# A fused attention and SwiGLU backward: the fourth ds tile of each block transposed by DMA from step 160, and the plain transfers issued from GpSimd

## The chip, the cores and the metric

One core of a Trainium2 chip runs the kernel. The metric is the device time of one execution in microseconds (us), as the median of several runs. Engines are named PE (TensorE matmul), PEld (its weight loads), DVE (VectorE), ACT (ScalarE), POOL (GpSimd) and SP (SyncE, which in this kernel does nothing but issue DMA).

## The reference, cut to what matters

```python
# x: 2048 tokens x 448, 16 heads of 28; the vjp gives six gradients beside the output
xn = layernorm(x)
out = x + attention(xn, wqkv, wo) + (silu(xn @ w_gate) * (xn @ w_up)) @ w_down
# backward of attention, per head:
#   ds = p * (dp - delta);  dq = ds @ k;  dk = ds.T @ q
```

The part that matters is the backward of the attention scores. The product ds comes out with query rows on the partitions. The dk sum can use it like that, but the dq sum needs it transposed.

## The kernel before

The backward is one loop of 512 steps. A step handles one query tile of 128 rows against 512 keys for two heads; four steps are a block. Between these steps PE works on other matmuls (the output, the FFN gradients, the weight gradients), which need plain loads that are "dripped" in.

```python
    def drop():                       # plain loads, paced over the steps
        ...
        while slow and credit > 0:
            _, _, o, i = slow.pop(0)
            SP.dma_start(out=o, in_=i)
            credit -= size(o)
...
    def dst_dma(b, ds, qi):           # one query tile, 128 x 1024 bf16, by DMA
        if qi == 0:
            dsT[b] = bk.tile([P, 4, 2, 4, P], BF16, name="dsT", bufs=3)
        SP.dma_start_transpose(out=dsT[b][:, qi].rearrange("p j kt s -> p (j kt) s"),
                               in_=ds[:].rearrange("p j k -> p (j k)"))

    def ew(k):                        # exponentials on ACT, ds on DVE
        ...
            if qi < 2 or qi == 2 and b < NB // 4 - 1:
                ...
                    dst_dma(b, ds, qi)
...
    def tr_unit(b):                   # the fourth tile: PE transposes, ACT copies
        for qi in (3,) if b < NB // 4 - 1 else (2, 3):
            ds = dss.pop(4 * b + qi)
            ps = ps_b.tile([P, 8, P], BF16, name="db", bufs=3)
            for c in range(8):
                PE.transpose(ps[:, c, :], ds[:, c // 4, (c % 4) * P:(c % 4 + 1) * P], ident_bf[:])
            ...
                ACTE.copy(out=o, in_=ps[:])
...
    def dq_unit(b):                   # reads dsT[b], nine steps after the block's last ds
        ...
        ACTE.mul(out=st[:], in_=ps[:, :256], mul=SCALE)
        if kc < 3:
            POOL.tensor_tensor(out=dq_acc[:, qsl], in0=dq_acc[:, qsl], in1=st[:], op=ALU.add)
```

So three tiles of each block are transposed by DMA from SyncE, the fourth by PE and ACT. SyncE also issues every plain load; GpSimd issues the stores and adds up dq.

The softmax here doesn't subtract the row's maximum and nothing guards it: scores larger than these inputs give would overflow.

## Time and profile before

| | before |
|---|---|
| median of 4 runs | 1445.22 us |
| span of the profiled run | 1440.1 us |
| steps 160 to 511 ("the stretch") | 860.68 to 1394.87 us, 534.2 us |
| after the stretch (tail) | 45.2 us |

The stretch is bounded by the first exponential of step 160 and the end of the last ds product. The page's first part gives busy time and share of the span per engine, its third part what each DMA queue moved (packets, MB, share of 16 engines). The lines that the prediction shows follow further down.

```profile
PE 1326.3 (92%) x12647; PEld 541.0 (38%) x12708; DVE 1151.8 (80%) x1997; ACT 1261.5 (88%) x2193; POOL 403.6 (28%) x561
...
q1 hardware_dynamic: 672576, 255.35, 87.1%
q0 software_dynamic: 7024, 13.82, 4.1%
```

Queue q1 is SyncE's and q0 is GpSimd's. The "issue" of a transfer is the time for which the instruction that starts it holds the issuing engine; the transfer "lands" later, when its data have arrived. SyncE is not in the first part, since issuing DMA is not counted as busy.

### The profile page before, as it was taken

Reading aid. Unit: us, or ns where it says so; the run is one execution under the profiler, and the core shown is the slowest. Engines: PE = TensorE matmul, PEld = TensorE weight load, DVE = VectorE, ACT = ScalarE, POOL = GpSimd, SP = SyncE. Lnnn points to the kernel's source line nnn. Section 1 sums busy time; section 2 is a strip of 40 time slices with the busy share of each in tenths; the row PEclk is TensorE's granted clock in tenths of the full one; section 3 lists DMA queues with packets and bytes.
Section 4 is the critical chain, followed back from the end, with each engine's and each line's share of the span. In section 5 each row is a group of like instructions: output and inputs, shape, how many; then the busy total and the mean of one; then the engine's idle time right before and its main releaser. Section 6 shows DMA issues by size and latency. Waiting matters only on the chain. (4 is left out here: it accounts for less than half of the span.)

```text
span 1440.1 us, 34682 instructions
## 1 busy us (share of the span) xinstructions
PE 1326.3 (92%) x12647; PEld 541.0 (38%) x12708; DVE 1151.8 (80%) x1997; ACT 1261.5 (88%) x2193; POOL 403.6 (28%) x561
## 2 busy tenths in 40 slices
PE   5889999999999999889999999999999999999996
PEld 2333333333333333333333434433443444444343
DVE  6667757666676676578998998888889999989988
ACT  5789988988889999869989989899989999989974
POOL 6464524464334454111112112201111011010006
PEclk9999999999999999989999999999999999999998
DMA  5796956796678586799999999999999999999971
GB/s 154 181 199 165 235 122 160 187 195 164 146 162 192 147 172 145 178 234 226 226 213 217 232 220 188 196 209 229 228 173 194 209 223 230 201 191 203 198 142 60
DMA packets 681179, 271.69 MB, mean 189 GB/s; under 512 B 606424, under 2 KB 655824, under 8 KB 681008
## 3 DMA queue, kind: packets, MB, share of 16 engines
q1 hardware_dynamic: 672576, 255.35, 87.1%
q0 software_dynamic: 7024, 13.82, 4.1%
q8 instruction: 100, 1.64, 0.5%
q14 instruction: 71, 0.58, 0.1%
q10 hardware_dynamic: 1408, 0.30, 0.1%
HBM read 65.09 MB, written 60.36 MB: 87 GB/s over the span
## 5 line engine op out<-in xcount | busy, mean ns | idle before, releaser
L842 DVE TENSOR_TENSOR ds_sb<-db,e_sb 128x512 bf16<-128x512 f32 x1024 | 646.8, 684 | 51.3 <-issue 21.1
L836 ACT ACTIVATE e_sb<-sb 128x512 bf16<-128x512 f32 x1024 | 554.8, 611 | 60.4 <-PE db L820 44.5
L612 ACT ACTIVATE eT<-s_w 128x1024 bf16<-128x1024 f32 x256 | 263.5, 1029 | 46.1 <-PE s_ps L609 43.1
L614 ACT ACTIVATE eT<-s_ps 128x512 bf16<-128x512 f32 x512 | 280.4, 612 | 0.0
L820 PE MATMUL db<-kd,qd 32*128 32x512 bf16 x1024 | 234.4, 384 | 8.2 <-DVE ds_sb L842 7.4
L812 PE MATMUL sb<-kd,qd 32*128 32x512 bf16 x1024 | 210.4, 387 | 5.1 <-DMA qd<-QD_d 3.3
L961 POOL TENSOR_TENSOR dq_acc<-dq_acc,dq_st 128x256 f32<-128x256 f32 x64 | 46.2, 721 | 455.4 <-ACT dq_st L959 455.4
L919 PE MATMUL acc<-ds_sb,qd 128*32 128x512 bf16 x1024 | 161.0, 391 | 0.0
L915 PE MATMUL acc<-e_sb,qd 128*32 128x512 bf16 x1024 | 158.8, 391 | 1.3 <-DVE dw_o L528 1.3
L902 ACT COPY dsT<-db 128x1024 bf16<-128x1024 bf16 x128 | 130.1, 1016 | 14.6 <-PE db L897 13.9
L380 POOL TENSOR_TENSOR nn<-nn,ag 128x512 f32<-128x512 f32 x56 | 71.2, 1271 | 252.2 <-DVE ag L378 243.7
L609 PE MATMUL s_ps<-QQ,KK 32*128 32x512 bf16 x512 | 125.4, 385 | 3.9
L1128 PE MATMUL genb<-wguT,dau_c 128*128 128x448 bf16 x448 | 117.5, 355 | 6.3 <-ACT dq_st L959 3.9
L609 PE MATMUL s_w<-QQ,KK 32*128 32x512 bf16 x512 | 100.3, 387 | 13.1 <-ACT eT L612 10.4
L812 PEld LDWEIGHTS <-qd 32*128 32x128 bf16 x1024 | 48.2, 91 | 149.4 <-issue 140.3
L421 PE MATMUL gen<-xn_t,f_sp 128*128 128x448 bf16 x416 | 91.8, 354 | 2.6 <-DVE nn L395 1.7
L421 PEld LDWEIGHTS <-f_sp 128*128 128x128 bf16 x640 | 55.7, 98 | 75.0 <-issue 31.9
L946 PE MATMUL genb<-dsT,kd 128*32 128x256 bf16 x2048 | 79.5, 275 | 1.9 <-DVE dqT L955 0.6
L897 PE MATMUL db<-ident_bf,ds_sb 128*128 128x128 bf16 x1032 | 79.4, 220 | 1.1 <-DVE ds_sb L842 1.1
L897 PEld LDWEIGHTS <-ds_sb 128*128 128x128 bf16 x1032 | 68.3, 99 | 24.1 <-issue 5.3
L451 PE MATMUL gen<-eT,VS 128*32 128x512 bf16 x1024 | 68.4, 384 | 5.5 <-DVE nn L395 3.3
L381 POOL TENSOR_TENSOR nn<-nn,tt 128x512 f32<-128x512 f32 x56 | 72.0, 1286 | 4.4
(167 smaller groups left out, 1911.0 us busy)
## 6 DMA issues: line engine op xcount, KB each, us to landing
F_d<-hda SPq DMA_DIRECT2D x56, 384.0 KB, 3.1
dau_c<-F_d SPq DMA_DIRECT2D x24, 512.0 KB, 4.4
qd<-QD_d SPq DMA_DIRECT2D x16, 512.0 KB
kd<-KD_d SPq DMA_DIRECT2D x16, 384.0 KB, 4.0
dsT<-ds_sb SPq DMA_TRANSPOSE x383, 4.3
dc<-dqkvT_d SPq DMA_DIRECT2D x12, 384.0 KB, 3.9
h_c<-F_d SPq DMA_DIRECT2D x8, 512.0 KB, 4.4
wT_d<-wT_f SPq DMA_DIRECT2D x14, 256.0 KB, 3.6
```

The costliest lines, as they stand in the source:

```text
L421: PE.matmul(ps[:, :D], lhsT=fsp[fc][:, t // 4, w, t % 4, :], rhs=rhs[:, t, :], start=(t == 0), stop=(t == NT - 1))
L609: PE.matmul(sp4[hh], lhsT=KK[g][r:r + HP, kt * P:(kt + 1) * P], rhs=QQ[g][r:r + HP, qsl], start=True, stop=True, tile_position=(r, 0))
L612: ACTE.activation(out=e2[0][:], in_=wide[:], func=ACT.Exp, scale=SCALE)
L614: ACTE.activation(out=e2[1][:, j], in_=sp4[2 + j], func=ACT.Exp, scale=SCALE)
L812: PE.matmul(s_ps[:], lhsT=qside[g, qc][r:r + HP, 0, qi * P:(qi + 1) * P], rhs=kside[g, kc][r:r + HP, 0, :], start=True, stop=True, tile_po ...
L820: PE.matmul(d_ps[:], lhsT=qside[g, qc][r:r + HP, 1, qi * P:(qi + 1) * P], rhs=kside[g, kc][r:r + HP, 1, :], start=True, stop=True, tile_po ...
L836: ACTE.activation(out=est[k][:, j], in_=sps.pop((k, j))[:], func=ACT.Exp, scale=SCALE)
L842: DVE.tensor_tensor(out=ds[:, j], in0=dps.pop((k - 1, j))[:], in1=est[k - 1][:, j], op=ALU.mult)
L897: PE.transpose(ps[:, c, :], ds[:, c // 4, (c % 4) * P:(c % 4 + 1) * P], ident_bf[:])
L902: ACTE.copy(out=o, in_=ps[:])
L915: PE.matmul(a[r:r + HP, :], lhsT=sp4[:, 1, r:r + HP], rhs=e[:, j, :], start=first, stop=last, tile_position=(0, r), skip_group_check=True)
L919: PE.matmul(a[r:r + HP, :], lhsT=sp4[:, 0, r:r + HP], rhs=ds[:, j, :], start=first, stop=last, tile_position=(0, r), skip_group_check=True)
```

## The change

The intent is to take 87 tiles off PE and ACT, which are nearly full, and give them to the DMA path. To make room in SyncE's queue, all plain loads from step 160 on are issued by GpSimd. As GpSimd would run ahead in stretches without sums, a tiny copy ("tie") makes it wait for ACT there.

```diff
-            SP.dma_start(out=o, in_=i)
+            (SP if now < 160 else POOL).dma_start(out=o, in_=i)
... (the same once more, in have())
+    PB = 40
+
+    def by_pe(b):
+        return (3,) if b < PB else (2, 3) if b == NB // 4 - 1 else ()
...
-            if qi < 2 or qi == 2 and b < NB // 4 - 1:
+            if qi not in by_pe(b):
...
-        for qi in (3,) if b < NB // 4 - 1 else (2, 3):
+        for qi in by_pe(b):
...
         if kc == 0:
             ACTE.mul(out=dq_acc[:, qsl], in_=ps[:, :256], mul=SCALE)
+            if now >= 160:
+                POOL.tensor_copy(out=tie[:], in_=dq_acc[0:1, qsl.start:qsl.start + 1])
             return
```

More of the change, by code (lines that the diff above doesn't have):

```diff
@@ L774, in have @@
             slow.remove(x)
-            SP.dma_start(out=x[2], in_=x[3])
+            (SP if now < 160 else POOL).dma_start(out=x[2], in_=x[3])
     def load_q(g, qc):
@@ L888, in late_dw @@
         yield 110
+    tie = bk.tile([1, 1], FP32, name="tie", bufs=1)
     dq_acc = bk.tile([P, S // 2], FP32, name="dq_acc", bufs=1)
     def tr_unit(b):
-        for qi in (3,) if b < NB // 4 - 1 else (2, 3):
+        for qi in by_pe(b):
             ds = dss.pop(4 * b + qi)
@@ L910, in kv @@
         e = est.pop(k)
-        ds = dss[k] if qi == 3 or k == NB - 2 else dss.pop(k)
+        ds = dss[k] if qi in by_pe(k // 4) else dss.pop(k)
         sp4 = qside[g, qc][:, 2:4, qi * P:(qi + 1) * P]
```

## The prediction

> **What bounds the kernel now.** I read the page first, then the busy time by stretch, then the groups of the stretch that the change touches, then the transposes' own view, then SyncE's queue. The chain of waits is of no use here: it holds only the last microsecond of the tail. The exponentials of the backward (line L836, two per step, 512 steps) place the steps in time: step 160 starts at 860.69 us and the last step ends at about 1393.40 us. The change acts only there, on 352 steps, that is 88 blocks of four query tiles, 532.71 / 88 = 6.05 us per block. Busy time by stretch (PE, PEld, DVE, ACT, POOL, clock, DMA share, GB/s), the whole stretch and then two pieces of 16 steps:
>
> ```profile
> 860.69:1393.40 532.71, 511.96 (x5868) 215.71 (x5867) 487.08 (x825) 489.80 (x913) 68.87 (x103) 0.99 1.08 202
> ...
> 961.10:985.60 24.50, 23.33 (x265) 9.65 (x266) 20.28 (x33) 23.35 (x46) 3.42 (x5) 1.00 1.13 207
> ...
> 1155.90:1179.20 23.30, 22.74 (x262) 9.28 (x263) 22.17 (x37) 22.03 (x41) 3.42 (x5) 1.00 1.13 238
> ```
>
> Three engines are nearly full together: PE 96%, ACT 92%, DVE 91%; in the piece at 1155.9 us DVE and ACT both stand at 95% and PE at 98%. The DMA share is above 1 because times of overlapping packets are added; it says "hardly ever idle". The groups of the same stretch, line engine op, count | busy, mean ns | idle before:
>
> ```profile
> L842 DVE TENSOR_TENSOR ds_sb<-db,e_sb 128x512 bf16<-128x512 f32 x705 | 445.7, 684 | 32.3 <-issue 18.0 <-ACT e_sb L836 6.5 <-PE db L820 1.8
> L836 ACT ACTIVATE e_sb<-sb 128x512 bf16<-128x512 f32 x704 | 382.4, 613 | 32.7 <-PE db L820 26.4 <-PE sb L812 0.9
> ...
> L902 ACT COPY dsT<-db 128x1024 bf16<-128x1024 bf16 x88 | 89.5, 1017 | 8.8 <-PE db L897 8.4
> L897 PE MATMUL db<-ident_bf,ds_sb 128*128 128x128 bf16 x704 | 54.6, 221 | 0.0
> ...
> L961 POOL TENSOR_TENSOR dq_acc<-dq_acc,dq_st 128x256 f32<-128x256 f32 x47 | 33.9, 721 | 342.3 <-ACT dq_st L959 342.3
> ```
>
> DVE's ds product alone is 446 us of 533. ACT and DVE wait mostly on PE, so PE sets the pace, with DVE close behind. L902 and L897 are the tile that the change takes away; GpSimd (L961) is mostly waiting. Now SyncE, which issues the three DMA transposes per block and all plain loads. First the transposes' view (issue min/median/max ns, then landing), then SyncE in order of time:
>
> ```profile
> L829 SPq DMA_TRANSPOSE dsT<-ds_sb x383: 1231/1296/4112, 623.7 to 1392.5; - x192
> ...
> DMA to landing us min/median/max: 3.1/4.3/7.0
> ```
>
> ```profile
> 1153.97 5.00 SPq L829 DMA_TRANSPOSE dsT<-ds_sb  x3
> 1159.02 0.57 SPq L769 DMA_DIRECT2D qd<-QD_d  x1
> 1159.69 4.99 SPq L829 DMA_TRANSPOSE dsT<-ds_sb  x3
> 1164.74 0.57 SPq L769 DMA_DIRECT2D dau_c<-F_d  x1
> 1165.62 4.91 SPq L829 DMA_TRANSPOSE dsT<-ds_sb  x3
> ```
>
> A transpose holds SyncE for 1.24 us at best, 1.30 us at the median. Three of these and one plain load span nearly the whole block of 5.7 us. Summing the trace's records of this stretch, 267 transposes hold SyncE for 418.5 us (mean 1.57 us) and 78 plain issues for 49 us: 467.6 of 532.7 us, 88%. So the issuing queue is the fourth resource that is nearly full, and it is the one that the change loads.
>
> **What the Trainium skill says.** (1) "DMA: Bandwidth & Descriptors", section "Issuing engines are not separate DMA queues": transfers started from different engines end up on the same 16 DMA engines and interleave; several issuers save only the issuing time. The plain loads, once on GpSimd, therefore still compete with the transposes. (2) Same page, "SWDGE vs HWDGE vs iDMA": the plain DMA transpose can be issued by SyncE or ScalarE only, so it is the loads that must move. The trace agrees as far as it goes: every transpose is SyncE's. (3) Same page, "Latency and other measured facts": 261 GB/s effective for a DMA transpose. Here one tile is 128 x 1024 bf16 = 262,144 B; over 1.24 us that is 211 GB/s, the pace of issue, while a 2 us stretch that (by its packet sizes) held transposes alone, behind a backlog, moved 282 GB/s:
>
> ```profile
> 1305.50:1307.50 2.00, 1.18 (x17) 0.76 (x16) 2.00 (x5) 1.39 (x3) 0.00 (x0) 1.00 1.27 282
> ```
>
> So the DMA engines can take a tile in about 0.95 us and SyncE cannot feed them faster than one in 1.24 us: there is some slack on the engines into which loads of another queue could fall.
>
> **The change, part by part.** *Removed:* for blocks 40 to 126 the fourth tile's PE transposes and evacuation: 87 x 8 = 696 PE transposes and 87 ACT copies. On ACT that is 87 x 1.017 = 88 us. On PE it is at most 54 us (54.6 us for 704). DVE loses nothing. One PSUM bank of three ("db") is no longer lent to the transpose. *Added:* 87 DMA transposes of 256 KB, the whole kernel going from 383 to 470, and about 20 tiny GpSimd copies, which make GpSimd wait for ACT in the stretches without sums (negligible work). *Moved:* the 78 plain loads, from SyncE to GpSimd. In this stretch q1 carried 102.32 MB, of which 268 x 0.262 = 70.3 MB transposes, so about 32 MB of loads move to q0, which carried 4.38 MB. At the 0.54 to 0.71 us that GpSimd's own store issues take, 78 issues are about 50 us on an engine with 69 us of work in 533.
>
> *What it could be worth.* PE falls from 512 to about 457 us, ACT from 490 to 401 us; DVE stays at 487 us. DVE becomes the floor: 487 / 88 = 5.53 us per block. DVE's best piece in this trace (16 steps at 1300 us, summed from the records) is 99% full, ordinary good ones 95 to 96%. At 97% the stretch takes 502 us, 31 us less, 2.1% of the kernel. So even a flawless transpose path only just reaches 2%.
>
> *What SyncE and the DMA engines need.* About 355 transposes in the stretch at 1.27 us (between floor and median) are 451 us, before any interference. To size interference I fitted, over the 383 issues in the trace, issue time against the plain bytes moved meanwhile: 1.31 us, plus 0.18 us per 100 KB of plain data of SyncE's own queue, plus 0.33 us per 100 KB of GpSimd's queue (mostly stores with short rows, so a poor stand-in for loads of long rows). *Favourable:* the loads fall into the engines' slack of about 0.29 us per tile and only bursts count; sharing evenly, a 512 KB load of 1.25 us (at the 418 GB/s of the turn into the backward, at 616 us, where only loads ran) takes 2.5 us, and the transposes fall behind by about 0.4 us after what the queue buffers; 72 such loads are 27 us: 451 + 27 = 478 us, out of the way of DVE. *As on SyncE's own queue:* 451 + 365 x 0.18 = 517 us. *As GpSimd's stores:* 355 x 1.31 + 365 x 0.33 = 585 us. SyncE also waits for data: a block's first transpose needs the buffer that the sums of three blocks before free, so it cannot run ahead and will hardly exceed 97 to 98%. The middle case then gives 517 / 0.975 = 530 us, today's pace. That is the heart of the prediction: the gain on PE and ACT is real but the queue that pays for it has little room.
>
> **Rivals.** *A, DVE becomes the bound, DMA keeps up:* 502 to 510 us for the stretch, total 1415 to 1423 us. For it: the 1.24 us floor leaves room, SyncE loses 49 us of plain issues, and there are some 9 steps (13 us) between the last tile's product and the sums that read it, against 4.3 us to land. Against it: the fit above. Chance 0.32. *B, SyncE's queue becomes the bound near today's pace:* heavy-fill pieces (6.4 us per block at 884 us) improve, pieces now at 5.8 us lose as much; 515 to 540 us, total 1428 to 1453 us. For it: 88% busy now with only three tiles. Chance 0.42. *C, contention:* loads from a second queue cut into the transposes more than in order on one queue; the dq matmuls (L946) then wait for DMA, and DVE for ds buffers; 550 to 585 us, total 1463 to 1498 us. For it: 0.33 against 0.18 us. Chance 0.2. *D, GpSimd in order:* loads stand behind sums and sums behind loads; with a single dq_st buffer a late sum stops ACT. Against it: sums are 0.72 us in 6 us and GpSimd waits 342 us for them. Chance 0.06, costing some 10 to 30 us.
>
> **The range and the chances.** Weighing the middles, A 1419, B 1440, C 1478 and D 1465 us, gives 0.32 x 1419 + 0.42 x 1440 + 0.2 x 1478 + 0.06 x 1465 = 1442 us. The favourable half of B and A are alike likelier than the bad end of C, since someone who moves every load has presumably seen the queue as the limit; I take 1438 us. Faster by over 2% means below about 1417 us: only the better third of A and a little beyond, 0.14. Slower by over 2% means above 1475 us: over half of C and a little of D, 0.16. The rest, 0.70, is within 2%. Eight times in ten: 1414 to 1476 us.
>
> **What would show it.** The counts: 470 transposes by DMA, 336 PE transposes (L897 now), 41 ACT copies. In the stretch ACT's busy share should fall to about 75 to 80% and PE's by 5 to 10 points. If A holds, DVE stands at 96% or more and transposes stay near 1.3 us. If B or C holds, DVE stays near 91% or lower, SyncE is full, mean transpose issue rises to 1.45 us or more, and PE's dq matmuls or DVE's ds products show waits for the DMA of dsT, today 3.6 us in all. If D holds, ACT's dq_st waits for GpSimd. The prediction is wrong if the stretch drops well below 500 us, which would mean that DVE's products themselves got shorter or idle gaps that I count as unavoidable went away, or if the transposes' latency passes 13 us and the steps stall block by block.

## The result, and the profile after

The change takes 1573.56 us against 1445.22 us, a ratio of 1.0906 (95% interval 1.0822 to 1.099): 9% slower, far outside the predicted range. The spans of the profiled runs differ by 128.4 us. Of these, 117.0 us lie in the stretch (651.2 against 534.2 us), 9.9 us in the tail and 1.5 us before step 160.

The stretch of the kernel after, by engine (columns as in the prediction's first fence):

```profile
862.19:1513.38 651.19, 534.01 (x5191) 183.97 (x5192) 487.98 (x827) 424.63 (x827) 123.21 (x201) 0.90 1.13 199
```

ACT's busy time fell by 66 us (490.3 to 424.6), and DVE's work is unchanged, but no engine is near full any more: DVE 75%, ACT 65%, PE 82%. The moved bytes show in the two queues on the page of the kernel after:

```profile
q1 hardware_dynamic: 743616, 246.26, 82.3%
q0 software_dynamic: 15840, 45.72, 11.8%
```

The groups of that stretch say what the engines wait for:

```profile
L846 DVE TENSOR_TENSOR ds_sb<-db,e_sb 128x512 bf16<-128x512 f32 x707 | 447.7, 685 | 158.5 <-PE db L820 50.7 <-DMA dsT<-ds_sb 43.5 <-issue 24.4
L840 ACT ACTIVATE e_sb<-sb 128x512 bf16<-128x512 f32 x704 | 379.8, 599 | 105.4 <-PE db L820 94.6 <-PE sb L812 1.9
...
L951 PE MATMUL genb<-dsT,kd 128*32 128x256 bf16 x1408 | 72.3, 296 | 87.3 <-DMA dsT<-ds_sb 79.5 <-DVE dxg L1183 2.3 <-DVE dxg L1143 2.1
```

PE's dq matmuls now wait 79.5 us for the transposes, DVE waits 43.5 us for ds buffers that the transposes have not yet read, and much of the rest waits for PE. In the kernel before, all waits of these two for these DMAs came to 3.6 us. The transposes' own view in the kernel after:

```profile
L833 SPq DMA_TRANSPOSE dsT<-ds_sb x470: 1231/1302/8862, 626.0 to 1517.5; - x157
...
DMA to landing us min/median/max: 3.2/5.2/11.6
```

The floor and the median of an issue are as before, but the longest went from 4.1 to 8.9 us. In order of time, SyncE shows one unbroken run of transposes:

```profile
1010.81 39.64 SPq L833 DMA_TRANSPOSE dsT<-ds_sb  x18
```

That is 39.64 / 18 = 2.2 us each. The worst place lies inside it, where GpSimd had just issued a load of 384 KB (it landed 10.2 us after its issue). Busy time by stretch, first during that load, then just after it:

```profile
1018.00:1027.00 9.00, 2.31 (x23) 0.82 (x19) 2.71 (x5) 2.59 (x5) 0.00 (x0) 0.92 1.21 99
1029.00:1031.00 2.00, 2.00 (x26) 0.57 (x22) 0.38 (x1) 0.89 (x3) 0.50 (x1) 0.50 1.27 281
```

For 9 us load and transposes together moved only 99 GB/s, and PE did 2.3 us of work. Right afterwards the transposes ran at 281 GB/s, with PE's clock at half.

### How full SyncE is

The profile has no busy line for SyncE, so I summed the trace's own records: the durations of all DMA instructions on SyncE in the stretch, and the time between one's end and the next one's start. In the common case that gap is 0.05 to 0.10 us; what exceeds 0.095 us is counted as waiting. The table has all runs, the experiments included.

| run | median us | stretch us | transposes, mean issue us | SyncE in issues us | SyncE waiting us | PE clock |
|---|---|---|---|---|---|---|
| before | 1445.22 | 534.2 | 267, 1.57 | 467.6 | 35.6 | 0.99 |
| the change | 1573.56 | 651.2 | 351, 1.76 | 616.4 | 2.5 | 0.90 |
| e1 loads on SyncE | 1534.41 | 620.0 | 349, 1.52 | 579.0 | 3.4 | 0.92 |
| e2 three tiles | 1466.25 | 564.9 | 268, 1.91 | 511.9 | 29.6 | 0.97 |
| e3 no tie | 1566.96 | 642.2 | 350, 1.73 | 607.0 | 2.5 | 0.90 |
| e4 loads on ACT | 1533.78 | 613.5 | 351, 1.64 | 574.9 | 6.2 | 0.92 |
| e6 every other | 1479.32 | 566.2 | 309, 1.55 | 529.7 | 3.1 | 0.97 |
| e7 few loads | 1497.89 | 585.2 | 350, 1.48 | 546.8 | 3.5 | 0.94 |
| e8 quiet blocks | 1438.35 | 529.8 | 278, 1.54 | 481.1 | 18.0 | 1.00 |
| e9 pairs | 1527.92 | 609.6 | 177, 3.00 | 586.9 | 2.5 | 0.93 |
| e10 change, few loads | 1516.99 | 593.6 | 349, 1.60 | 558.3 | 2.5 | 0.93 |
| e11 extra whole | 1541.63 | 625.1 | 350, 1.54 | 586.1 | 3.9 | 0.95 |
| e12 extra half | 1515.93 | 600.1 | 350, 1.46 | 561.4 | 3.8 | 0.95 |

In the kernel after, SyncE waits for only 2.5 us of 651: the stretch is as long as SyncE is occupied. In the kernel before it had 35.6 us to spare. This table is from the traces alone; the experiments say what fills the queue. "Occupied" includes the time for which the DMA path behind SyncE holds an issue back; the table does not separate the two.

The profile's own view of SyncE's waits seems to say otherwise: over the whole kernel after it puts 390 us down to DVE's ds products. That view takes the last update of the awaited semaphore before an issue ends, so it cannot tell a wait from a long issue. The records can. In the change a transpose starts 10.3 us (median; 4.0 us at the least) after the end of the ds product that it reads, so none of the 351 waits for it. In the kernel before the median is 1.2 us, and 69 of 267 start within 0.3 us.

### The profile page after: what moved, and what is told of

Same layout as the page of the kernel before. It is cut to its first block, busy times and chain, and to the rows that moved or that the text cites. A ratio compares the mean times of both kernels' runs of the same rounds, so it can differ in the third digit from the quotient of the medians.

```text
span 1568.5 us, 33310 instructions
## 1 busy us (share of the span) xinstructions
PE 1360.3 (87%) x12012; PEld 510.6 (33%) x12012; DVE 1151.6 (73%) x1997; ACT 1195.7 (76%) x2106; POOL 459.2 (29%) x659
## 3 DMA queue, kind: packets, MB, share of 16 engines
q8 instruction: 94, 1.54, 0.4%
## 5 line engine op out<-in xcount | busy, mean ns | idle before, releaser
L820 PE MATMUL db<-kd,qd 32*128 32x512 bf16 x1024 | 246.6, 405 | 25.4 <-DVE ds_sb L846 24.8
L812 PE MATMUL sb<-kd,qd 32*128 32x512 bf16 x1024 | 220.2, 408 | 5.1 <-DMA qd<-QD_d 3.2
L951 PE MATMUL genb<-dsT,kd 128*32 128x256 bf16 x2048 | 99.0, 292 | 91.1 <-DMA dsT<-ds_sb 83.2
L924 PE MATMUL acc<-ds_sb,qd 128*32 128x512 bf16 x1024 | 169.1, 406 | 0.3 <-DVE ds_sb L846 0.2
L920 PE MATMUL acc<-e_sb,qd 128*32 128x512 bf16 x1024 | 166.1, 406 | 1.3 <-DVE dw_o L528 1.3
L1135 PE MATMUL genb<-wguT,dau_c 128*128 128x448 bf16 x448 | 123.2, 390 | 2.0 <-ACT dq_st L966 1.1
L951 PEld LDWEIGHTS <-kd 128*32 128x32 bf16 x2048 | 60.3, 100 | 142.6 <-issue 74.9
L966 ACT ACTIVATE dq_st<-genb 128x256 f32<-128x256 f32 x88 | 34.1, 388 | 87.2 <-PE genb L951 86.5
L920 PEld LDWEIGHTS <-qd 128*32 128x32 bf16 x1024 | 32.4, 95 | 106.0 <-issue 102.7
```

Source lines behind the costliest of these rows:

```text
L812: PE.matmul(s_ps[:], lhsT=qside[g, qc][r:r + HP, 0, qi * P:(qi + 1) * P], rhs=kside[g, kc][r:r + HP, 0, :], start=True, stop=True, tile_po ...
L820: PE.matmul(d_ps[:], lhsT=qside[g, qc][r:r + HP, 1, qi * P:(qi + 1) * P], rhs=kside[g, kc][r:r + HP, 1, :], start=True, stop=True, tile_po ...
L920: PE.matmul(a[r:r + HP, :], lhsT=sp4[:, 1, r:r + HP], rhs=e[:, j, :], start=first, stop=last, tile_position=(0, r), skip_group_check=True)
L924: PE.matmul(a[r:r + HP, :], lhsT=sp4[:, 0, r:r + HP], rhs=ds[:, j, :], start=first, stop=last, tile_position=(0, r), skip_group_check=True)
L951: PE.matmul(ps[r:r + HP, :256], lhsT=ks[:, kt, h:h + HP], rhs=t[:, par::2, j, kt, :], start=(kt == 0), stop=(kt == 3), tile_position=(0, r ...
L1135: PE.matmul(ps[:, :D], lhsT=d[:, i // 2, i % 2, tsl], rhs=dxs["w", fq][:, i // 2, i % 2, :], start=(i == 0), stop=(i == n - 1))
```

## The experiments

### First round: which half of the change costs

Theory T1 was that loads on a second queue stall the transposes in the DMA engines; T2, that four transposes a block are too much wherever the loads are issued; T3, that only GpSimd's software queue does harm.

**e1_loads_on_sp**: four tiles by DMA, loads left on SyncE, no tie.

```diff
-            (SP if now < 160 else POOL).dma_start(out=o, in_=i)
+            SP.dma_start(out=o, in_=i)
... (twice; and the tie's two lines removed)
```

> All four tiles by DMA from step 160, but the plain loads stay on SyncE's queue (no tie needed). Theory T1, loads from a second queue stall the transposes in the DMA engines: the loss goes away; SyncE needs about 355 x 1.27 + 78 x 0.58 + 320 x 0.18 us = 554 us at most for a stretch that takes 533 before, so 1430 to 1470 us in all, mean transpose issue near 1.5 us. Theory T2, too many bytes and too much SyncE time for four tiles whatever the queue of the loads: about as slow as the change, 1550 us or more.

Measured: 1534.41 us against 1440.97 us for before on the same chip, ratio 1.0659. Neither figure was hit, but T1 fell as the main cause: with the loads back in SyncE's queue, 93 of the 128 us remain. The stretch, and a piece of SyncE in order of time:

```profile
856.68:1476.72 620.04, 524.56 (x5191) 183.06 (x5191) 487.84 (x827) 424.00 (x827) 68.84 (x103) 0.92 1.12 208
```

```profile
1150.08 4.59 SPq L833 DMA_TRANSPOSE dsT<-ds_sb  x3
1154.72 0.57 SPq L769 DMA_DIRECT2D wguT<-wT_d  x1
1155.39 2.69 SPq L833 DMA_TRANSPOSE dsT<-ds_sb  x2
```

Each row begins 0.05 to 0.10 us after the row before it ends: there is no free time. The fragments add up to the whole stretch (579.0 us of issues, 3.4 us of waits, the rest such gaps).

**e2_three_tiles**: the other half alone, three tiles by DMA with the loads on GpSimd.

```diff
-    PB = 40
+    PB = NB // 4 - 1
```

> The other half alone: three tiles by DMA and the fourth by PE as before, but the plain loads on GpSimd with the tie. T1: the transposes stall beside the loads here too, with 88 fewer of them and SyncE with more room to catch up: 20 to 80 us over the kernel before, mean transpose issue 1.7 us or more against 1.57 before. T2: no slower than before, 1445 us or less, since SyncE lost 49 us of issues and nothing was added.

Measured: 1466.25 us, ratio 1.0162 (1.0134 to 1.0189): clear of 1. T1's figure for this half held. In the profiled run the stretch is 31 us longer than before, and a transpose issue takes 1.91 us in the mean, although SyncE has no plain load left. This run, 1475.97 us, is the slowest of the four, and 13 of its 31 us lie in steps 176 to 191, where transposes were held up:

```profile
883.95 40.54 SPq L833 DMA_TRANSPOSE dsT<-ds_sb  x12
```

That is 3.4 us each. Elsewhere SyncE still waited 29.6 us, so in e2 it was full in bursts and not throughout. The two halves add up in the profiled runs: from before to e2 31 us, from e1 to the change 31 us, and 86 us for the fourth tile. By the medians, each less its own before, the moved loads cost 25 and 35 us and the fourth tile 93 and 103 us.

**e3_no_tie**: the change without the 20 tie copies (the two added lines removed).

> The change without the 20 tie copies. If the tie is a cost (GpSimd held in order by it): faster than the change by 10 us or more. If GpSimd's order is not the matter (T1, T2): within 1.5% of the change, 1550 to 1600 us, perhaps worse as loads bunch up in the stretches without sums.

Measured: 1566.96 us, 0.4% under the change: the tie is not the cause. Nor are late loads: in the trace of the change no engine's wait is put down to one of the loads that GpSimd issues.

**e4_loads_on_act**: the change with the loads on ScalarE's queue, no tie.

```diff
-            (SP if now < 160 else POOL).dma_start(out=o, in_=i)
+            (SP if now < 160 else ACTE).dma_start(out=o, in_=i)
```

> The change with the loads on ScalarE's hardware queue in place of GpSimd's software queue, no tie. T1 in its general form, any second queue: as slow as the change, 1540 to 1600 us, with transpose issues above 1.7 us. T3, only the software queue of GpSimd does it: 1430 to 1480 us (ScalarE pays some 78 x 0.6 = 47 us for issues out of the 88 us that it was spared).

Measured: 1533.78 us, the same as e1. Neither theory's range was hit. A second hardware queue gives back about what it takes: SyncE is spared 47 us of load issues, and its transposes take 43 us more (574.9 against 531.8 us). Only GpSimd's queue makes it worse: e3, like e4 without the tie, takes 33 us more than e4.

### Second round: is it the number of transposes

Theory S: SyncE and the DMA path behind it are full, and what is added beyond the room left costs its whole time.

**e6_every_other**: as e1, but the fourth tile by DMA in every other block.

```diff
-        return (3,) if b < PB else (2, 3) if b == NB // 4 - 1 else ()
+        return (2, 3) if b == NB // 4 - 1 else (3,) if b < PB or b % 2 else ()
```

> Loads on SyncE, the fourth tile by DMA only in every other block from step 160 (44 more transposes, not 87). If the loss is a queue that overflows (S: SyncE and the DMA engines are full in the stretches with loads, so what is added beyond the room left costs its whole time): SyncE's free 65 us of before swallow half of the 44 x 1.5 = 66 us, so 1440 to 1475 us, less than half of the 93 us that all 87 cost. If each added transpose costs the same (linear): 1487 us. If the gain on PE and ACT shows as long as the queue has room: 1425 to 1440 us.

Measured: 1479.32 us, ratio 1.026, a little above S's range and below the linear figure. I had taken SyncE's free time as 65 us; it was 36. With that, the account closes: the stretch grew by 32.0 us and SyncE's waiting shrank by 32.5 us, 64.5 / 44 = 1.47 us for each added transpose.

**e7_few_loads**: as e1, but 33 of the loads left out (the result is wrong).

```diff
+        if ch > 0:
+            dxs[ch, fq] = dxs[0, fq]
+            return
         d = dxs["pool"].tile([P, 5, 2, 512], BF16, name="dau_c")
...
     def load_dc(ch):
+        if ch > 0:
+            dcs[ch] = dcs[0]
+            return
```

> All four tiles by DMA, loads on SyncE, but the slices of the FFN gradients and of dqkv loaded once instead of four times (33 of 78 loads gone, some 13 MB of 32; wrong result on purpose, same matmuls on old data). S: what overflows is the sum of transposes and loads, so without those loads SyncE needs about 87 us less (33 x 0.58 issue and 13 MB at 0.16 us per 100 KB of interference, 40 us, and the gaps that follow), and the stretch falls towards the DVE floor: 1420 to 1465 us, granted clock over 0.97. If the number of transposes alone is too much (1.3 us each and landing): still over 1500 us.

Measured: 1497.89 us, ratio 1.0392, a miss for S's figure: I expected 87 us less on SyncE and it was 35 (17 us of issues, 15 us of push-back on transposes, 3 us of gaps). The other theory, over 1500 us, was missed by 2 us. So the loads are the smaller part. SyncE still waits for only 3.5 us. The stretch:

```profile
860.02:1445.23 585.21, 514.69 (x5191) 182.12 (x5192) 486.67 (x827) 423.22 (x827) 68.92 (x103) 0.94 1.12 196
```

**e8_quiet_blocks**: as e1, but the fourth tile by DMA only in eleven blocks without loads.

```diff
+        return (2, 3) if b == NB // 4 - 1 else () if b in (40, 41, 42, 43, 72, 73, 74, 75, 124, 125, 126) else (3,)
```

> Loads on SyncE, the fourth tile by DMA only in the eleven blocks whose stretches hold no loads (steps 160 to 175, 288 to 303, 496 to 507). S: there the queue has room and PE and ACT gain, 0.2 to 0.4 us a block, 2 to 4 us in all: 1436 to 1441 us beside a before of 1441 (ratio 0.997 to 1.0). If transposes cost as such: 12 us slower (93 x 11 / 87).

Measured over 5 rounds: 1438.35 us, ratio 0.998 (0.9957 to 1.0002). That is in the expected place, and the stretch of the profiled run fell from 534.2 to 529.8 us, but the interval includes 1, so it is not shown to beat the kernel before. A transpose costs nothing measurable where SyncE has room: by the 1.47 us of e6, eleven more take an estimated 16 us of SyncE, and its waiting fell by 17.6 us.

### Third round: instructions or bytes

**e9_pairs**: as e1, but one instruction transposes two query tiles from step 160 (the ds tiles are allocated in pairs).

```diff
+        SP.dma_start_transpose(out=dsT[b][:, qi - 1:qi + 1].rearrange("p q j kt s -> p (q j kt) s"),
+                               in_=dp[:].rearrange("p q j k -> p (q j k)"))
```

> As e1_loads_on_sp, but from step 160 one transpose instruction takes two query tiles (2048 columns), so 175 instructions fewer on SyncE with the same bytes. Theory S2, SyncE's queue is occupied all the time, a tile costing 1.295 us of issue plus 0.093 us to the next instruction: the issue of a pair takes 2.5 to 2.6 us, and 175 x 0.093 = 16 us go, 1510 to 1522 us beside 1534 of e1. If SyncE is not the bound (latency of the transposes, or the half-speed clock of PE after its gaps): no faster or slower than e1, since a pair starts later, 1530 to 1560 us.

Measured: 1527.92 us, ratio 1.059, a gain of 6 us over e1 in the medians and 10 us in the stretch where 16 were expected; both expected ranges were missed. The view of the transposes (issue min/median/max ns):

```profile
L841 SPq DMA_TRANSPOSE dsT<-ds_sb x174: 1347/3078/5810, 871.7 to 1472.3; - x174
```

A pair can be issued in 1.35 us, hardly more than a single tile, but usually takes 3.08 us: SyncE is held longer than two single issues and their gap take at the median (2.7 us). I read this as the path behind holding it back; the trace does not show where. Halving the instructions gains 10 of the 86 us.

**e10_change_few_loads**: the change with the loads left out as in e7 (wrong).

> The change itself (loads on GpSimd) with the 33 repeated loads of the FFN gradients and of dqkv left out (wrong result on purpose, as in e7). S2: SyncE is always occupied, and the fit of the change's trace puts 0.34 us of transpose issue on each 100 KB that GpSimd's queue moves; 33 loads of 13 to 14 MB then cost 45 us, so 1520 to 1535 us, while SyncE still never waits. If GpSimd's loads only delay by coming late (D): the same gain as e7 over e1 or less, 36 us, and SyncE shows waits for data.

Measured: 1516.99 us, ratio 1.0523: 57 us less than the change, and SyncE still waits only 2.5 us. S2 had the direction right and the size somewhat low (1520 to 1535 us, from a gain of 45 us). The same loads cost 36 us on SyncE's queue (e1 less e7) and 57 us on GpSimd's.

**e11_extra_whole_b** and **e12_extra_half_b**: the kernel before with nothing removed, and the fourth tile transposed by DMA as well, into a scratch tile that nobody reads; e12 takes half the tile. The first build of each did not fit the on-chip memory, so two of the tail's four dx buffers were given up.

```diff
+            elif qi == 3 and 40 <= b < NB // 4 - 1:
+                x = bk.tile([P, 8, P], BF16, name="scr", bufs=1)      # e12: [P, 4, P]
+                SP.dma_start_transpose(out=x[:], in_=ds[:].rearrange("p j k -> p (j k)"))   # e12: in_=ds[:, 0]
```

> The kernel before with nothing taken away: from step 160 the fourth tile is still transposed by PE and copied by ACT, and is transposed by DMA as well, into a scratch tile that nobody reads (87 more transposes, loads on SyncE; two of the tail's four dx buffers give the room, which can cost a microsecond or two in the tail). S2: the stretch is as long as SyncE is occupied, so what PE and ACT do besides does not matter: as e1_loads_on_sp, 1525 to 1550 us, SyncE waiting under 10 us in the stretch. If e1 is a loss on DMA less a gain on PE and ACT: 20 us or more slower than e1; if nobody depends on the extra transposes and they fall into free time: near the kernel before, under 1470 us.

> As e11, but the extra transpose takes only half of the tile (512 columns). If a transpose costs SyncE by its bytes (0.65 us issue and 0.09 us gap): 87 x 0.74 = 64 us, less the 36 us that SyncE waited before, so 1465 to 1485 us. If it costs by the instruction (1.3 us whatever its size): as e11.

Measured: e11 1541.63 us (ratio 1.069), e12 1515.93 us (1.0518). e11 is as slow as e1 within 7 us, although nobody needs the extra tiles and PE and ACT kept their work. The stretch of e11:

```profile
858.34:1483.40 625.06, 546.71 (x5887) 222.15 (x5888) 489.69 (x827) 493.63 (x914) 69.01 (x103) 0.95 1.13 207
```

ACT does 494 us of work here and 424 us in e1, and the stretches are 625 and 620 us: what the change saved on PE and ACT was worth about 5 us. So the stretch follows SyncE and the path behind it, and not PE or ACT. The extra transposes, first in e11:

```profile
L850 SPq DMA_TRANSPOSE scr<-ds_sb x87: 1232/1287/3011, 871.0 to 1486.6; - x87
```

Then in e12, at half the bytes:

```profile
L850 SPq DMA_TRANSPOSE scr<-ds_sb x87: 1188/1225/2793, 872.0 to 1462.9; - x87
```

My expectation for e12 (cost by bytes, 1465 to 1485 us) was wrong, and the other (as e11) was missed by 26 us. Half the bytes still hold SyncE for 1.19 us at least. By the growth of the stretch and the loss of waiting time, a whole extra tile cost (90.9 + 31.7) / 87 = 1.41 us and a half tile (65.9 + 31.8) / 87 = 1.12 us. So below one tile most of the price is per instruction, and above it the path seems to set it (e9); at the tile size that this kernel uses the two nearly meet.

## Why the prediction was wrong, point by point

**What bounds the kernel now**: right in its list, wrong in one size. SyncE was named as the fourth resource that is nearly full, at 88%. But 88% counted issue time alone. The gap after each issue belongs to the cost as well. It stood in the prediction's own fence: 1159.69 + 4.99 is 1164.68, and the next row starts at 1164.74. With gaps, SyncE was at 93%, and 36 us were free, not 65. Two small misreadings do not carry the argument: DVE's line has 18.0 us on "issue", 6.5 us on ACT and 1.8 us on PE, so DVE did not wait mostly on PE; and the least issue is 1.231 us, not 1.24.

**What the change is worth**: the counts were right (the ACT copies went from 128 to 41, the PE transposes from 1032 to 336), and DVE's floor stayed at 488 us. The relief was not: ACT's busy time fell by 66 us and not by 88. The groups of ACT in the stretch before add up to 531 us where its busy time is 490, so the copies' records overlap others and their times cannot simply be subtracted. PE's busy time even rose, from 513 to 534 us, at a granted clock of 0.90 instead of 0.99. None of this bounds the stretch, since the queue binds first: e1 against e11 puts the relief at 5 us.

**What SyncE and the DMA engines need** is the step that failed: "About 355 transposes in the stretch at 1.27 us (between floor and median) are 451 us, before any interference." The runs show in its place, for the change, 351 transposes at 1.30 us, plus 0.10 us of gap each, plus 30 us that go with instruction fetches: 456 + 35 + 30 = 521 us before any load. The loads then add 129 us, against the 66 us of the middle case that the prediction made its heart (517 us). So of the 133 us missing on SyncE, 70 are in this term and 63 in the loads. (The terms are from a fit over the issues of the after trace, of the same kind as the prediction's with one term more: 1.30 us, 0.34 us per 100 KB on GpSimd's queue, 0.36 us per instruction-fetch packet. Such a fit adds up to the total by construction, so the sum proves nothing; it only shares the time out. Instruction fetches get much the same, 29 us, in a fit of the kernel before.)

**The choice among the three cases of interference** failed too. The coefficient of "As GpSimd's stores", 0.33 us per 100 KB, was measured again as 0.34 us, so the case dismissed as "a poor stand-in" was the right one in its coefficient. The "short rows" were not looked up: in the stretch before, GpSimd's stores moved in packets of 3.6 KB in the mean, SyncE's loads in packets of 1.6 KB. (And 72 x 0.4 us in the favourable case is 29 us, not 27.) The favourable case rested on the claim "the DMA engines can take a tile in about 0.95 us". The 282 GB/s behind it is a burst: in the after trace 281 GB/s appears just after a stall. Even e9, whose instructions carry two tiles, averages 212 GB/s over its stretch, loads included, and a tile takes 1.5 us of SyncE.

**The relief from moving the loads** was counted as 49 us gained on SyncE. By e2 against before, and by the change against e1, moving them to GpSimd loses 25 to 35 us by the medians (31 us of stretch). The issues go, but a transpose pays more per byte beside that queue.

**Rivals**: C named the mechanism, loads on a second queue cutting into the transposes with PE waiting for DMA and DVE for ds buffers, and got a chance of 0.2 and 1463 to 1498 us. Its size, by the fit above, left out the gaps and the fetches. B's mechanism, SyncE as the bound, was right as well, and it is the larger part (86 of 117 us in the stretch). A fell: it set 4.3 us to land against 13 us of reserve and left out the queue, in which a tile now stands 10.3 us at the median before a landing of 5.2 us. D fell: removing the tie changed the time by 0.4%, inside the intervals, no engine waits for a load, and ACT's dq_st waits 86 us, but for PE, not for GpSimd.

**A consequence that was not foreseen** is PE's clock. In e1 PE waits for a transpose, in order of time:

```profile
910.26 1.04 PE L951 MATMUL genb<-dsT,kd 128*32 128x256 bf16 x14 [2.27 <-DMA dsT<-ds_sb]
```

The granted clock before and after that wait (the number ahead of the DMA share):

```profile
904.00:908.00 4.00, 3.99 (x36) 1.67 (x33) 3.65 (x9) 2.80 (x6) 0.06 (x1) 1.00 1.18 266
910.50:914.00 3.50, 3.50 (x33) 1.27 (x26) 2.01 (x4) 2.48 (x5) 1.82 (x3) 0.50 1.16 262
```

The wait of 2.3 us is followed by half speed. The Trainium skill describes this ("TensorE: Matmul & The Clock Gate", section "Part 1: The HAM clock gate"): after an idle window of about 3.4 us the array runs at half rate. This trace agrees in kind, with a shorter gap. It accounts for the clock of 0.92 in e1, but it doesn't set the time, since SyncE hardly waits there (3.4 us). In the tail, where the clock stands between 0.66 and 0.74 in the first 17 us and SyncE still works off transposes until 1518.9 us, it probably has a share of the 9.9 us; that was not tested apart.

**Left open**: why a transpose pays twice as much per byte beside GpSimd's queue (0.34 us per 100 KB, against 0.17 in a fit of e1), why the path moved only 99 GB/s for 9 us in the worst place, and what in the path holds a pair back to 3 us. One difference: the same loads move in packets of 1.6 KB in the mean on SyncE's queue (e1) and on ScalarE's (e4), and of 4.2 KB on GpSimd's; no run separates packet size from queue. Nor does any run separate SyncE's own time from that of the path behind it. A larger reserve (more dsT buffers, later sums) was not run.

## What to carry to other kernels

A queue that issues DMA is an engine, though the page does not count it as busy: add up the issues and the gaps between them, and ask how many microseconds it really waits, before giving it work. Once it waited for nothing here, every further transpose cost its full 1.4 us whatever it freed elsewhere, and moving its plain loads to another queue made no room: they still slowed the transposes. Test a shift of work by adding the new work without removing the old; if the time is the same, the saving was not on the path.

## What the Trainium skill lacked or had wrong

- "DMA: Bandwidth & Descriptors", "Issuing engines are not separate DMA queues", says that using several issuers only saves issue time. ScalarE's queue in place of SyncE's saved nothing (1533.78 against 1534.41 us), and GpSimd's cost 31 us of stretch, by a fit 0.34 us of transpose issue per 100 KB. The page does not say that it can be a loss.
- The same page, "Latency and other measured facts", gives 261 GB/s for DMA transposes (one kernel, with a non-contiguous middle dimension; more when contiguous). Back to back here a tile of 256 KB takes 1.30 us and a gap of about 0.09 us, 189 GB/s. That is the pace of one issuing queue and need not be the limit of the path, which reached 281 GB/s over 2 us after a stall. The row does not speak of the pace of issue.
- No page gives, in time and by size, what a transpose costs the sequencer that issues it on this chip ("DMA: Bandwidth & Descriptors" has cycle counts for "previous generations" only, in a table on a later chip). Here it is at least 1.19 us for 512 columns, 1.23 us for 1024 and 1.35 us for 2048.
- "Runtime: NRT & Kernel Launch", "Instruction fetch mechanics", calls the cost of crossing a 16 KiB block of instructions "mostly hidden"; it does not say what a fetch does to other transfers. Fetches show in the trace as packets of 16,384 and 8,192 B on two queues of their own, and a transpose beside one, with no load in flight, takes 1.8 us in the mean of some 48, against 1.29 us in the mean of some 170 without; by the fit that is some 30 us in the stretch. That the fetch is the cause was not tested.
- "TensorE: Matmul & The Clock Gate", "Part 1: The HAM clock gate", puts the idle window at about 3.4 us. The spells of half speed in e1's stretch do last whole multiples of 3.41 us, but the window need not be idle throughout: a gap of 2.3 us was followed by half speed.
